# Where an attention pair's operand preparation stands in three instruction streams

## The chip, the cores and the metric

The kernel runs on one core of one Trainium2 chip. The metric is the device time of one execution in microseconds. Each core has a matmul engine (PE, with its weight loads PEld), VectorE (DVE), ScalarE (ACT), GpSimd (POOL) and a queue engine, SyncE (SP), which here only issues DMAs. Every engine works through its own instruction stream in order; semaphores join the streams.

## The reference

Causal attention with a decay, then a mixture of experts (one expert per token), then a two-layer network. Only the first part is touched by the change.

```python
B, H, S, D = q.shape                      # 4, 8, 576, 64
scores = scale * np.matmul(q, k.transpose(0, 1, 3, 2))
log_f = np.log(np.clip(f, 0.0001, 1.0))
cum = np.cumsum(log_f, axis=-1)
decay = cum[:, :, :, None] - cum[:, :, None, :]
causal = np.triu(np.ones((S, S), dtype=bool), k=1)
scores = np.where(causal, -1000000000.0, scores + decay)
scores = scores - np.max(scores, axis=-1, keepdims=True)
attn = np.exp(scores)
attn = attn / (np.sum(attn, axis=-1, keepdims=True) + 1e-09)
return np.matmul(attn, v).astype(np.float32)
# then: x = _moe_ref(x, ...); return _moe2_ref(x, w_in, w_out)
```

## The kernel before

The 32 heads are worked on in 16 **pairs** of heads, `g` = 0 to 15, in one loop of 17 turns. Turn `g` computes the scores of pair `g` and finishes pair `g-1`. Below, "pair 9" also means the turn that begins with pair 9's first scores.

**Operands.** The scores need about full single precision from a matmul that takes a rounded type, so each operand is split into a high part (rounded) and a low part (the rest). `raw` holds q in partitions 0 to 63 and k in 64 to 127. `prep_hi(g)` makes the high part on DVE (L299, `aq <- raw, qs`), issues two small loads of decay rows (L301, L302) and a copy of k's high part into `bk` (L303), all on SP, and two copies on POOL (L305). `prep_lo(g)` copies k's high part into the upper half of `ak` on ACT (L312, `ak <- aq`), makes the low part on DVE (L313, `raw <- raw, qs, aq`), issues three SBUF-to-SBUF DMAs of 288 KB on SP (L314 `bq <- raw`, L315 `ak <- raw`, L316 `aq <- aq`) and one copy on POOL (L317). L316 writes q's high part over the place where k's high part stood in `aq`, so it must come after L303, L312 and L313 have read it, and the first scores of that pair must wait until it has landed.

**One turn** is written as four stages, and with `ordered(tc, MS)` PE, ACT, DVE and SP keep the order in which they are written; POOL's order is set by a scheduler.

- `first(g)`: scores of query blocks 0 and 1 on PE and their maxima on DVE (L341, `nm`); transposes of pair g-1's block 3 on PE (L420, two PSUM tiles `pt`), their copies to SBUF on ACT (`cs`, L422); `prep_lo(g + 1)`; `store`, which issues finished rows of the attention output to DRAM on SP (L549, L551); the exponentials of blocks 0 and 1 on ACT (L346).
- `last(g)`: scores of the fifth, half block; the transposes of pair g-1's fifth block and their two copies on ACT (L412); pair g-1's first product with v (`pv`, L432) and its copy on DVE (L438); the fifth block's exponential on ACT (L393).
- `third(g)`: scores of block 2, the other `pv`, the exponentials of block 2, the transposes and copies of blocks 0 and 1.
- `fourth(g)`: scores of block 3; the loads of `raw` for pair g+3 (L202) and of `v` for pair g+1 (L193) on SP; `prep_hi(g + 2)`; transposes and copies of block 2; `xout(g - 1)`, the output stage; the exponentials of block 3.

`xout` scales pair g-1's output. It has two halves: matmuls into a PSUM tile `xo` (L455), then on DVE two products that read it (L459, into `x` and `lp`).

**PSUM.** The tiles `pt`, `xo` and `rk` share three buffers in turn, so each needs the third tile before it to have been read. The second `pt` tile of block 3 takes the buffer of the first `xo`, and the first `pt` tile of the fifth block that of the second `xo`. The scores have two buffers `sc` in turn: block 2's scores wait for the exponentials of blocks 0 and 1, block 3's for those of the fifth block.

**Side work.** After each four pairs the tokens of one batch are routed to experts in many small DVE instructions (`routed`, lines 473 to 536), whose first ones run in turns 5, 9 and 13, and after that the batch's rows are stored, one `store` a turn: 513 KB (L551) in turns 7, 8, 11 and 12, 128 KB (L549) in turns 9 and 13. In turn 2, `gload(1)` issues six small loads (L166, L170 four times, L171), written between `first` and `last`.

Of the kernel before, what the change touches and what calls it, by code (L numbers as in the profile page):

```python
# [9 lines left out]
F32 = mybir.dt.float32  # L10
# [9 lines left out]
P = 128  # L20
# [53 lines left out]
def fused(ctx: ExitStack, tc, qk0, qk2, vp, f, mid, wg, mb, w1, w2, w_in, w_out, out):  # L74
    nc = tc.nc
# [70 lines left out]
    with tc.tile_pool(name="pst", bufs=PST, space=PSUM) as pst:  # L146
# [40 lines left out]
        ops = {}  # L187
# [17 lines left out]
        NBUF = 2  # L205
        bqs = [pre.tile([68, 2, S], F32R, name=f"bq{i}") for i in range(NBUF)]
        bks = [pre.tile([68, 2, S], F32R, name=f"bk{i}") for i in range(NBUF)]
# [86 lines left out]
        def prep_hi(g):  # L294
            raw = ops[g]
            aq, ak = (aqk.tile([P, 2, S], F32R, tag=n, name=f"{n}{g}") for n in ("aq", "ak"))
            h = aq.bitcast(F32)
            bq, bk, a4, b4 = bqs[g % NBUF], bks[g % NBUF], aq4[g % NBUF], bq4[g % NBUF]
            nc.vector.tensor_scalar(aq, raw, qs, None, ALU.mult)  # L299
            for t, r0, c0 in ((bq, 64, 0), (bk, 66, 2)):  # L300
                nc.sync.dma_start(t[r0:r0 + 2].bitcast(F32), agd[c0:c0 + 2, 2 * g:2 * g + 2, :])  # L301
            nc.sync.dma_start(b4[64:66, :, :64].bitcast(F32), agd[0:2, 2 * g:2 * g + 2, 4 * P:])  # L302
            nc.sync.dma_start(bk[0:64].bitcast(F32), h[64:128])  # L303
            for r in (0, 64):
                nc.gpsimd.tensor_copy(a4[r:r + 64, :, :64], h[0:64, :, 4 * P:])  # L305
            ops[g] = (raw, aq, ak)

        def prep_lo(g):
            raw, aq, ak = ops[g]
            bq, bk, b4 = bqs[g % NBUF], bks[g % NBUF], bq4[g % NBUF]  # L310
            h = aq.bitcast(F32)
            nc.scalar.copy(ak[0:64], h[64:128])  # L312
            nc.vector.scalar_tensor_tensor(raw.bitcast(F32R), raw, qs, h, ALU.mult, ALU.subtract)  # L313
            nc.sync.dma_start(bq[0:64].bitcast(F32), raw[0:64])  # L314
            nc.sync.dma_start(ak[64:128].bitcast(F32), raw[64:128])  # L315
            preps.append(nc.sync.dma_start(h[64:128], h[0:64]))  # L316
            nc.gpsimd.tensor_copy(b4[0:64, :, :64], raw[0:64, :, 4 * P:])  # L317
            ops[g] = (aq, bq, ak, bk)

        st = {}  # L320
        XA, XB = 3 * P, P + 64
# [81 lines left out]
        def tr(g, c, js):  # L403
            sb = part_of(g, c // 3)
            if c == 4:
                pt = st.pop((g, c, "p"))
                for b0, b1 in ((0, 3), (3, 5)):
                    ps = pst.tile([P, 512], F32, tag="t", name=f"pt{g}_4_{b0}")
                    for b in range(b0, b1):
                        nc.tensor.transpose(ps[:, (b - b0) * P:(b - b0 + 1) * P], pt[:, b * P:(b + 1) * P], ident)  # L410
                    i = ps[:, :(b1 - b0) * P].rearrange("p (b j q) -> p j b q", j=2, q=64)
                    nc.scalar.copy(sb[:, :, b0:b1, P:], i)  # L412
                return
            pt = st[g, c, "p"]
            ps = pst.tile([P, 512], F32, tag="t", name=f"pt{g}_{c}_{js[0]}")
            nb = c + 1
            for i, j in enumerate(js):
                for b in range(nb):
                    k = i * nb + b
                    nc.tensor.transpose(ps[:, k * P:(k + 1) * P], pt[:, j, b * P:(b + 1) * P], ident)  # L420
            o = sb[:, js[0]:js[-1] + 1, 0:nb, c % 3 * P:(c % 3 + 1) * P]
            return lambda: nc.scalar.copy(o, ps[:, :len(js) * nb * P].rearrange("p (j b q) -> p j b q", b=nb, q=P))  # L422
# [14 lines left out]
            st[g, "x", part] = xu  # L437
            nc.vector.tensor_copy(xu[:, :w], pv_[:, :w])  # L438

        def xout(g):  # L440
            b, gg = divmod(g, H // 2)
            if gg == 0 and b:
                xt[b] = (pe, pre)[b % 2].tile([P, NC, XW], F32, tag="x", name=f"x{b}")
            x = xt[b]
            lp = lps[b % 2]
            rr = a3.tile([P, NC, 2], F32, tag="rr", name=f"rr{g}")

            nc.vector.tensor_copy(sms[g % 3][:64, 4, 1:2], sms[g % 3][64:, 4, 0:1])
            nc.vector.tensor_scalar(rr, sms[g % 3], 1e-9, None, ALU.add)
            nc.vector.reciprocal(rr, rr)  # L450
            for part, c0, n in ((0, 0, 3), (1, 3, 2)):
                xu = st.pop((g, "x", part))
                ps = pst.tile([P, 512], F32, tag="t", name=f"xo{g}_{part}")
                for i in range(n):
                    nc.tensor.matmul(ps[:, i * HW:(i + 1) * HW], lhsT=xu[:, i * P:(i + 1) * P], rhs=idw[:, gg, :], start=True, stop=True)  # L455
                i0 = ps[:, :n * HW].rearrange("p (c d) -> p c d", d=HW)
                sc = rr[:, c0:c0 + n, :].unsqueeze(3)
                for o, a, w in ((x[:, c0:c0 + n, gg * P:(gg + 1) * P], slice(0, P), D), (lp[:, c0:c0 + n, gg, :], slice(P, HW), E)):
                    nc.vector.tensor_tensor(o.rearrange("p c (j d) -> p c j d", j=2), i0[:, :, a].rearrange("p c (j d) -> p c j d", j=2), sc.to_broadcast([P, n, 2, w]), ALU.mult)  # L459
            if gg == H // 2 - 1:  # L460
                routing.append(route(b))
                if b == B - 2:
                    routing.append(route1(pre, (B - 1) * NC))
# [179 lines left out]
        NG = BH // 2  # L643
# [4 lines left out]
        def routed(n=1):  # L648
            for _ in range(n):
                if routing and next(routing[0], 1):  # L650
                    routing.pop(0)


        def first(g):
            then = qk01(g) if g < NG else None
            cs = [tr(g - 1, 3, (j, )) for j in range(2)] if g else ()
            if g + 1 < NG:
                prep_lo(g + 1)
            store(1 + (g > 12))
            for c in cs:  # L660
                c()
            for _ in then or ():
                pass

        def last(g):
            then = qk4(g) if g < NG else None
            if g:
                tr(g - 1, 4, (0, 1))
                routed()
                pv(g - 1, 0)  # L670
                routed(2 + (g > 12))
            if then:
                then()
# [12 lines left out]
        def fourth(g):  # L686
            then = qk(g, 3) if g < NG else None
            if g + 3 < NG:
                load(g + 3)
            if g + 1 < NG:  # L690
                vload(g + 1)
            if g + 2 < NG:
                prep_hi(g + 2)
            cs = [tr(g, 2, (j, )) for j in range(2)] if then else ()
            for c in cs:
                c()
            if g:
                xout(g - 1)
            if then:
                then()  # L700

# [530 lines left out]
```

## Time and profile before

| | us |
|---|---|
| median of 3 runs | 893.01 |
| lowest and highest | 888.86, 893.55 |
| the profiled execution, its own time | 889.86 |
| its span, first to last instruction | 888.2 |

The attention pairs lie in the first 205 us or so, the experts and the last network behind them. Times in the rows are microseconds from the first instruction of the span. A row of the time line has the start, the duration, the engine, the line, what is written and read with its size, and how many instructions are merged; in brackets stands the idle time of the engine before it and who ended it.

### The profile page before, as it was taken

Reading aid. Unit: us, or ns where it says so; the run is one execution under the profiler, and the core shown is the slowest. Engines: PE = TensorE matmul, PEld = TensorE weight load, DVE = VectorE, ACT = ScalarE, POOL = GpSimd, SP = SyncE. Lnnn points to the kernel's source line nnn. Section 1 sums busy time; section 2 is a strip of 40 time slices with the busy share of each in tenths; the row PEclk is TensorE's granted clock in tenths of the full one; section 3 lists DMA queues with packets and bytes.
Section 4 is the critical chain, followed back from the end, with each engine's and each line's share of the span. In section 5 each row is a group of like instructions: output and inputs, shape, how many; then the busy total and the mean of one; then the engine's idle time right before and its main releaser. Section 6 shows DMA issues by size and latency. Waiting matters only on the chain. (4 is left out here: it accounts for less than half of the span.)

```text
span 888.2 us, 14348 instructions
## 1 busy us (share of the span) xinstructions
PE 853.8 (96%) x4733; PEld 704.4 (79%) x4733; DVE 601.7 (68%) x1070; ACT 503.7 (57%) x969; POOL 124.9 (14%) x185
## 2 busy tenths in 40 slices
PE   5999999998999999999999999999999999999996
PEld 4788787886788788888787788888888888888885
DVE  6678777886748999999985373386337943473333
ACT  5787778776348899999975353453223422242221
POOL 5000000001112314532231000000000000001112
PEclk9999999999999999999999999999999999999998
DMA  5776786766278145121322240032001300011111
GB/s 153 222 175 183 204 201 180 203 174 221 74 229 285 53 155 166 55 71 51 107 96 64 59 143 13 1 106 84 1 1 48 119 24 0 1 48 48 48 47 72
DMA packets 32994, 92.91 MB, mean 105 GB/s; under 512 B 7349, under 2 KB 8021, under 8 KB 32914
## 3 DMA queue, kind: packets, MB, share of 16 engines
q1 hardware_dynamic: 28082, 76.70, 29.8%
q0 software_dynamic: 4800, 15.23, 5.4%
q8 instruction: 39, 0.64, 0.3%
q14 instruction: 41, 0.34, 0.1%
q10 hardware_dynamic: 32, 0.01, 0.0%
HBM read 132.09 MB, written 14.99 MB: 166 GB/s over the span
## 5 line engine op out<-in xcount | busy, mean ns | idle before, releaser
L1124 ACT COPY us<-u 128x512 f32<-128x512 f32 (+1 forms) x80 | 43.6, 544 | 162.6 <-PE u L1122 162.5
L1125 DVE SCALAR_TENSOR_TENSOR us<-u,us 128x512 f32<-128x512 f32 (+1 forms) x80 | 51.0, 638 | 124.7 <-ACT us L1124 123.1
L1122 PE MATMUL u<-fxl,whii 128*128 128x512 f32 (+1 forms) x320 | 118.0, 369 | 0.0
L1122 PE MATMUL u<-fxh,wloi 128*128 128x512 f32 (+1 forms) x320 | 117.9, 368 | 0.0
L1122 PE MATMUL u<-fxh,whii 128*128 128x512 f32 (+1 forms) x320 | 116.8, 369 | 0.7 <-ACT fxh L764 0.7
L1142 PE MATMUL a<-whio,gh 128*128 128x512 f32 x280 | 109.6, 392 | 0.0
L1142 PE MATMUL a<-wloo,gh 128*128 128x512 f32 x280 | 109.2, 390 | 0.0
L1142 PE MATMUL a<-whio,gl 128*128 128x512 f32 x280 | 103.2, 389 | 0.0
L876 DVE TENSOR_TENSOR w1l<-w1r,w1h 128x1024 fp32r<-128x1024 f32 x72 | 86.3, 1221 | 10.8 <-ACT w1h L875 8.3
L346 ACT ACTIVATE p<-sc,nm 128x128 f32<-128x128 f32 (+3 forms) x128 | 66.2, 527 | 28.9 <-DVE nm L341 27.2
L876 DVE TENSOR_TENSOR w2l<-w2r,w2h 128x1024 fp32r<-128x1024 f32 x68 | 80.2, 1218 | 0.8 <-ACT w2h L875 0.7
L1127 ACT CAST gh<-us 128x512 fp32r<-128x512 f32 (+1 forms) x76 | 44.6, 587 | 58.1 <-DVE us L1125 38.5
L875 ACT CAST w1h<-w1r 128x1024 fp32r<-128x1024 f32 x72 | 73.7, 1055 | 3.6 <-PE h L893 3.6
L1128 DVE TENSOR_TENSOR gl<-us,gh 128x512 fp32r<-128x512 f32 (+1 forms) x76 | 49.3, 648 | 38.5 <-ACT gh L1127 36.4
L875 ACT CAST w2h<-w2r 128x1024 fp32r<-128x1024 f32 x68 | 69.5, 1052 | 4.4 <-PE y L921 2.3
L1122 PEld LDWEIGHTS u<-fxh,whii 128*128 128x128 f32 x320 | 60.2, 188 | 11.0 <-ACT fxh L764 0.9
L1122 PEld LDWEIGHTS u<-fxh,wloi 128*128 128x128 f32 x320 | 60.3, 188 | 10.3
L1122 PEld LDWEIGHTS u<-fxl,whii 128*128 128x128 f32 x320 | 60.3, 188 | 10.3
L341 DVE TENSOR_REDUCE nm<-sc 128x2 f32<-128x256 f32 (+1 forms) x64 | 51.1, 820 | 23.4 <-PE sc L337 21.3
L921 PE MATMUL y<-w2h,hh 128*128 128x512 f32 x160 | 64.8, 405 | 0.0
L1152 POOL DMA_INDIRECT out<-acc,tid x18 | 18.0, 997 | 326.0 <-DVE acc L1149 287.5
L921 PE MATMUL y<-w2h,hl 128*128 128x512 f32 x160 | 63.1, 395 | 0.2 <-DVE hl L914 0.2
(275 smaller groups left out, 1807.6 us busy)
## 6 DMA issues: line engine op xcount, KB each, us to landing
w1r<-w SPq DMA_DIRECT2D x88, 512.0 KB
w2r<-w SPq DMA_DIRECT2D x82, 512.0 KB
rwi<-w_in SPq DMA_DIRECT2D x16, 512.0 KB
rwo<-w_out SPq DMA_DIRECT2D x16, 512.0 KB
raw<-qk SPq DMA_DIRECT2D x14, 576.0 KB
vt<-vp SPq DMA_DIRECT2D x16, 320.0 KB
xr<-yd SPq DMA_DIRECT2D x18, 256.5 KB
bk<-aq SPq DMA_DIRECT2D x15, 288.0 KB
```

Source lines behind the costliest of these rows:

```text
L341: nc.vector.tensor_reduce(nm, view, axis=AX.X, op=ALU.max, negate=True)
L346: st["exp"] = nc.scalar.activation(pt[:, j, :], view[:, j, :], AF.Exp, bias=nm[:, j:j + 1], scale=1.0, accum_out=sms[g % 3][:, c, j:j + 1])
L875: nc.scalar.copy(hi[k], raw[k])
L876: nc.vector.tensor_tensor(lo[k], raw[k], hi[k].bitcast(F32), ALU.subtract)
L921: nc.tensor.matmul(Yp[t], lhsT=ap[:, k * P:(k + 1) * P], rhs=wp[k // 2][:, k % 2, :], start=(k == 0 and i == 0), stop=(k == NFB - 1 and i ...
L1122: nc.tensor.matmul(ps, lhsT=w[:, c], rhs=x[:, k, :], start=(k == 0 and i == 0), stop=(k == NKB - 1 and i == 2))
L1124: nc.scalar.copy(us, ps)
L1125: nc.vector.scalar_tensor_tensor(us, ps, 0.01, us, ALU.mult, ALU.max)
L1127: nc.scalar.copy(gh, us)
L1128: nc.vector.tensor_sub(gl, us, gh.bitcast(F32))
L1142: nc.tensor.matmul(A[b][i], lhsT=x[:, c], rhs=w, start=(first and m == 0), stop=(last and m == 2))
L1152: d = nc.gpsimd.indirect_dma_start(out=out[:, :], out_offset=bass.IndirectOffsetOnAxis(ap=tid[:, c:c + 1], axis=0), in_=Y[b, i], in_offset ...
```

## The change

The diff changes no instruction, only where three pieces of `prep_hi` and `prep_lo` stand:

1. `prep_lo` is parted. A new `prep_k` holds the ACT copy of `ak` and the DMA `aq <- aq`. For pairs 1 and 2 it follows `prep_lo` directly; for pairs 3 to 15 it stands in `last`, behind the copies of the fifth block.
2. From turn 2 on, `prep_lo` stands behind the copies `cs` of block 3.
3. `prep_hi(g + 2)` stands between the two halves of `xout(g - 1)`, where it stood ahead of both.

```diff
@@ prep_lo @@
-            nc.scalar.copy(ak[0:64], h[64:128])
             nc.vector.scalar_tensor_tensor(raw.bitcast(F32R), raw, qs, h, ALU.mult, ALU.subtract)
             nc.sync.dma_start(bq[0:64].bitcast(F32), raw[0:64])
             nc.sync.dma_start(ak[64:128].bitcast(F32), raw[64:128])
+            nc.gpsimd.tensor_copy(b4[0:64, :, :64], raw[0:64, :, 4 * P:])
+
+        def prep_k(g):
+            raw, aq, ak = ops[g]
+            h = aq.bitcast(F32)
+            nc.scalar.copy(ak[0:64], h[64:128])
             preps.append(nc.sync.dma_start(h[64:128], h[0:64]))
-            nc.gpsimd.tensor_copy(b4[0:64, :, :64], raw[0:64, :, 4 * P:])
-            ops[g] = (aq, bq, ak, bk)
+            ops[g] = (aq, bqs[g % NBUF], ak, bks[g % NBUF])
...
-        def xout(g):
+        def xout(g, between=None):
...
+                if part == 0 and between:
+                    between()
@@ first @@
-            if g + 1 < NG:
+            if g < 2:
+                prep_lo(g + 1)
+                prep_k(g + 1)
+            for c in cs:
+                c()
+            if 2 <= g < NG - 1:
                 prep_lo(g + 1)
             store(1 + (g > 12))
-            for c in cs:
-                c()
@@ last @@
                 tr(g - 1, 4, (0, 1))
+                if 2 <= g < NG - 1:
+                    prep_k(g + 1)
                 routed()
                 pv(g - 1, 0)
@@ fourth @@
-            if g + 2 < NG:
-                prep_hi(g + 2)
             cs = [tr(g, 2, (j, )) for j in range(2)] if then else ()
             for c in cs:
                 c()
+            hi = (lambda: prep_hi(g + 2)) if g + 2 < NG else None
             if g:
-                xout(g - 1)
+                xout(g - 1, hi)
+            elif hi:
+                hi()
```

On ACT, turn 2 before (from the exponentials of block 3 of pair 1 on; numbers at the end of names are buffers):

```order
L346 ACTIVATE p_3_530,sm_185<-sc_3_483,nm_3_490 128x512 x2
L312 CAST ak_497<-aq_496 64x1152
L422 COPY tt_1_548<-pt_3_0_549 128x4x128
L422 COPY tt_1_548<-pt_3_1_554 128x4x128
L346 ACTIVATE p_01_567,sm_186<-sc_01_533,nm_0_544 128x128 x2
L346 ACTIVATE p_01_567,sm_186<-sc_01_533,nm_1_546 128x256 x2
L412 COPY tt_1_548<-pt_4_0_590 128x2x3x64
L412 COPY tt_1_548<-pt_4_3_595 128x2x2x64
L393 ACTIVATE p_177,sm_186<-sc_4_578,nm_4_579 128x576
```

and after (lines behind the edit count some lines further):

```order
L350 ACTIVATE p_3_530,sm_185<-sc_3_483,nm_3_490 128x512 x2
L426 COPY tt_1_548<-pt_3_0_549 128x4x128
L426 COPY tt_1_548<-pt_3_1_554 128x4x128
L350 ACTIVATE p_01_565,sm_186<-sc_01_533,nm_0_544 128x128 x2
L350 ACTIVATE p_01_565,sm_186<-sc_01_533,nm_1_546 128x256 x2
L416 COPY tt_1_548<-pt_4_0_588 128x2x3x64
L416 COPY tt_1_548<-pt_4_3_593 128x2x2x64
L320 CAST ak_517<-aq_516 64x1152
L397 ACTIVATE p_177,sm_186<-sc_4_576,nm_4_577 128x576
```

The copy of `ak` has moved past eight instructions, to just ahead of the fifth block's exponential.

On DVE, from the maxima of block 3 in turn 2 to the low part in turn 3, before:

```order
L341 TENSOR_REDUCE nm_3_651<-sc_3_644 128x2
L299 TENSOR_SCALAR aq_657<-raw_492,qs 128x1152
L448 COPY sm_185<-sm_185 64x1
L449 TENSOR_SCALAR rr_676<-sm_185 128x10
L450 RECIPROCAL rr_676<-rr_676 128x10
L459 TENSOR_TENSOR x_209<-xo_0_680,rr_676 128x3x128
L459 TENSOR_TENSOR lp_191<-xo_0_680,rr_676 128x3x16
L459 TENSOR_TENSOR x_209<-xo_1_686,rr_676 128x2x128
L459 TENSOR_TENSOR lp_191<-xo_1_686,rr_676 128x2x16
L341 TENSOR_REDUCE nm_0_705<-sc_01_694 128x2
```

and after:

```order
L345 TENSOR_REDUCE nm_3_651<-sc_3_644 128x2
L452 COPY sm_185<-sm_185 64x1
L453 TENSOR_SCALAR rr_667<-sm_185 128x10
L454 RECIPROCAL rr_667<-rr_667 128x10
L463 TENSOR_TENSOR x_209<-xo_0_671,rr_667 128x3x128
L463 TENSOR_TENSOR lp_191<-xo_0_671,rr_667 128x3x16
L299 TENSOR_SCALAR aq_677<-raw_492,qs 128x1152
L463 TENSOR_TENSOR x_209<-xo_1_686,rr_667 128x2x128
L463 TENSOR_TENSOR lp_191<-xo_1_686,rr_667 128x2x16
L345 TENSOR_REDUCE nm_0_705<-sc_01_694 128x2
```

The high part (`aq`) now stands between the products of the first and of the second `xo`; all else keeps its order.

On SP, the end of `prep_lo` in turn 2, before:

```order
L314 DMA bq_174<-raw_350 64x1152
L315 DMA ak_497<-raw_350 64x1152
L316 DMA aq_496<-aq_496 64x1152
L166 DMA mbs<-mb 128x16
L170 DMA midi<-mid 128x4x2 x4
L171 DMA midi<-mid 64x4x2
L202 DMA raw_653<-qk 128x1152
```

and after:

```order
L313 DMA bq_174<-raw_350 64x1152
L314 DMA ak_517<-raw_350 64x1152
L166 DMA mbs<-mb 128x16
L170 DMA midi<-mid 128x4x2 x4
L171 DMA midi<-mid 64x4x2
L321 DMA aq_516<-aq_516 64x1152
L202 DMA raw_653<-qk 128x1152
```

`aq <- aq` (L316 before, L321 after) now stands behind `gload`'s six loads. In the six turns that store, it likewise stands behind the store, as in turn 7 before:

```order
L315 DMA ak_1333<-raw_1153 64x1152
L316 DMA aq_1332<-aq_1332 64x1152
L551 DMA xs<-x_209 128x2x513
L202 DMA raw_1484<-qk 128x1152
L193 DMA vt_1486<-vp 128x640
```

and after:

```order
L314 DMA ak_1353<-raw_1153 64x1152
L557 DMA xs<-x_209 128x2x513
L321 DMA aq_1352<-aq_1352 64x1152
L202 DMA raw_1484<-qk 128x1152
L193 DMA vt_1486<-vp 128x640
```

The store and `aq <- aq` have changed places. On PE and, apart from the copy of `ak`, on ACT nothing else moves; the order of POOL's copies is as before.

## Rows read from the trace of the kernel before

**Rows 1.** The page, busy time, share and instructions of PE over the span.

```profile
PE 853.8 (96%) x4733; PEld 704.4 (79%) x4733; DVE 601.7 (68%) x1070; ACT 503.7 (57%) x969; POOL 124.9 (14%) x185
```

**Rows 2.** Time line of PE, starts of stages in pairs 7, 8 and 9.

```profile
97.16 0.32 PE L331 MATMUL sc<-ak,aq 128*128 128x128 f32 x1
...
98.39 1.04 PE L420 MATMUL pt<-ident,p 128*128 128x128 f32 x8
99.18 0.51 PE L383 MATMUL sc<-ak,aq 128*128 128x288 f32 x2
...
108.66 0.32 PE L331 MATMUL sc<-ak,aq 128*128 128x128 f32 x1
...
120.58 0.32 PE L331 MATMUL sc<-ak,aq 128*128 128x128 f32 x1
...
121.80 0.60 PE L420 MATMUL pt<-ident,p 128*128 128x128 f32 x4
122.62 0.63 PE L420 MATMUL pt<-ident,p 128*128 128x128 f32 x4 [0.22 <-DVE lp L459]
123.00 0.52 PE L383 MATMUL sc<-ak,aq 128*128 128x288 f32 x2
...
126.68 0.44 PE L331 MATMUL sc<-ak,aq 128*128 128x384 f32 x1 [0.30 <-ACT p L346]
```

**Rows 3.** Waits of PE from 20 to 195: total us, times, longest.

```profile
PE pt L420 <- DVE lp L459: 2.0, 8, 0.4
PE sc L331 <- DMA aq<-aq: 1.4, 2, 0.9
PE sc L331 <- ACT p L346: 1.2, 4, 0.3
```

**Rows 4.** Time line of DVE in pair 9.

```profile
120.18 0.81 DVE L299 TENSOR_SCALAR aq<-raw,qs 128x1152 fp32r<-128x1152 f32 x1
...
122.27 0.20 DVE L459 TENSOR_TENSOR lp<-xo,rr 128x48 f32<-128x48 f32 x1
...
123.86 1.01 DVE L341 TENSOR_REDUCE nm<-sc 128x2 f32<-128x256 f32 x2
```

**Rows 5.** Time line of ACT in pair 9.

```profile
121.77 1.15 ACT L312 CAST ak<-aq 64x1152 fp32r<-64x1152 f32 x1
...
124.90 0.37 ACT L346 ACTIVATE p<-sc,nm 128x128 f32<-128x128 f32 x1 [1.02 <-DVE nm L341]
...
129.14 0.58 ACT L346 ACTIVATE p<-sc,nm 128x384 f32<-128x384 f32 x1 [1.13 <-DVE nm L341]
```

**Rows 6.** Time line of SP in pair 2, issues of `prep_lo` and `gload`.

```profile
41.81 0.74 SPq L316 DMA_DIRECT2D aq<-aq  x1
...
43.90 3.57 SPq L170 DMA_DIRECT2D midi<-mid  x4
47.52 0.71 SPq L171 DMA_DIRECT2D midi<-mid  x1
```

**Rows 7.** Time line of PE, first scores of pair 3.

```profile
48.24 0.30 PE L331 MATMUL sc<-ak,aq 128*128 128x128 f32 x1
```

**Rows 8.** Time line of SP in pair 8.

```profile
114.48 0.73 SPq L316 DMA_DIRECT2D aq<-aq  x1
115.26 1.24 SPq L551 DMA_DIRECT2D xs<-x  x1
```

**Rows 9.** DMA traffic from 113 to 121, all queues.

```profile
DMA packets 560, 1.65 MB, mean 206 GB/s; under 512 B 65, under 2 KB 65, under 8 KB 559
```

**Rows 10.** Busy times from 195 to 212; the last figure is DMA's GB/s.

```profile
195.00:212.00 17.00, 13.92 (x119) 10.84 (x117) 13.41 (x45) 13.15 (x34) 2.24 (x2) 1.00 0.84 301
```

**Rows 11.** Time line of SP in pair 0, the issue for pair 1.

```profile
19.19 0.46 SPq L316 DMA_DIRECT2D aq<-aq  x1
```

**Rows 12.** Time line of PE, first scores of pairs 1 and 14.

```profile
23.35 0.30 PE L331 MATMUL sc<-ak,aq 128*128 128x128 f32 x1 [0.95 <-DMA aq<-aq]
...
182.58 0.30 PE L331 MATMUL sc<-ak,aq 128*128 128x128 f32 x1 [0.43 <-DMA aq<-aq]
```

## The prediction

> **What bounds the kernel now.** The page comes first: PE is busy 96% of the span [rows 1], so what shortens the time is a wait of PE, and the change touches the attention pairs alone. Next the time line of PE, read by the first scores of each pair. Pair 7 runs from 97.16 to 108.66, 11.50 us, with no wait marked at the places shown; I take that as what PE needs. Pair 8 runs to 120.58, 11.92 us, 0.42 more [rows 2]. Where the 0.42 lies is seen one pair later, in the same stage: the eight transposes of block 3 take 0.79 us in pair 7 (98.39 to 99.18) and 1.20 in pair 9 (121.80 to 123.00), since the second four wait for DVE's product `lp`, which frees their PSUM buffer. The row calls 0.22 of this idle; start to start it is 0.41, and that is the price I use [rows 2].
>
> Then PE's waits by cause [rows 3]. Three kinds bear on the change. The wait for `lp` comes 8 times (pairs 2, 5, 6, 8, 9, 10, 12, 13). The wait of block 2's scores for ACT's exponentials comes 4 times; pair 9 shows one of 0.30 [rows 2]. The wait for the DMA `aq <- aq` (L316) comes twice, at the first scores of pairs 1 and 14. The last says that this DMA lands close to when it is needed.
>
> **The high part between the output halves (DVE).** The high part takes 0.81 us and stands ahead of the products; the first `lp` ends at 122.47 [rows 4]. Behind it, `lp` ends near 121.66, and the second four transposes could start at 121.80 + 0.40 = 122.20. The wait is gone, 0.41 in each of 8 pairs, 3.3 us at most. The second half's `lp` ends when it did, since DVE does the same work up to there, and its taker stands behind the fifth block's scores, which begin at 122.59 at the soonest: no new wait. The high part itself ends about 1.4 us later, and with it L303 and POOL's two copies; they are needed one pair (11.5 us) later, and SP has nothing behind L303 until the low part is made: nothing.
>
> Not all of the 3.3 reaches the end. In pairs 5, 9 and 13 routing lengthens DVE's stretch: the maxima of blocks 0 and 1 end at 124.87 [rows 4], the exponentials start at 124.90 after an idle 1.02 [rows 5], and block 2's scores wait for them until 126.68 [rows 2]. DVE's sum up to the maxima is unchanged, so PE would wait 0.71 there instead of 0.41 + 0.30: nothing gained. In pairs 6 and 10, which still do routing, I keep half, 0.2 each (an estimate). Pair 2 ends in another wait (below): nothing. Pairs 8 and 12 keep 0.41 each, if nothing else holds the next pair.
>
> **The copy of `ak` (ACT).** It takes 1.15 us. In pair 9 it stood where ACT then idled 1.02 anyway; now it stands where ACT idled 1.13 ahead of block 2's exponentials [rows 5]. The cover is 0.02 short; what those exponentials release (transposes) comes two PE stages later, so I cost it at nothing; without cover it would be 0.1 a pair over 13 pairs, 1.3 us. The copies of block 3 come about 1 us sooner, but the exponentials behind them wait for DVE: nothing, and below nothing only where DVE is early.
>
> **The DMA `aq <- aq` (SP).** This is where I expect the loss. It is now issued when the copy of `ak` has ended, about 1.1 us later than before in a plain pair (the copy's own 1.15), and behind whatever is written between. How near is it to its need? The only issue with little else queued ahead is pair 0's: issued at 19.19 [rows 11], released PE at 23.35 [rows 12], 4.16 us. In pair 8 it was issued at 114.48 [rows 8]; 4.16 us later is 118.64, and PE needed it at 120.58, so there the slack is at most 1.94 and, as no wait shows, at least 0. In the plain pairs (3 to 6, 10, 14) a delay of 1.1 fits into the upper end, and the two DMAs queued ahead of it delay its landing anyway: I take nothing, at most 0.4 in each of six pairs.
>
> *Pair 2.* SP issues `gload`'s six loads from the end of L316 to 48.23, about 5.6 us [rows 6]. L316, at 41.81 before, comes near 47.4; plus 4.16 is 51.6, and pair 3 began at 48.24 [rows 7]: 3.3 us lost. At the other end the four `midi` issues (3.57 us) go 1 us faster without L316's bytes ahead, and the landing takes 3 us on an empty queue (both estimates): 1.2 us. I take 2.0, nearer the lower end, since six loads of a few KB leave the queue empty. Pair 2's own 0.41 is swallowed by this wait.
>
> *Pairs 7, 8, 11, 12.* A store of 513 KB (0.525 MB) now goes ahead of L316. At the 301 GB/s of a dense stretch [rows 10] that moves L316 by 1.75 us, at the 206 GB/s of pair 8 [rows 9] by 2.55. In pair 8 the landing is then between 118.64 + 1.75 = 120.39 and 120.58 + 2.55 = 123.13, and without the `lp` wait it is needed at 120.17: PE waits 0.2 to 3.0, less the 0.41 gained, so -0.2 to +2.5; I take 1.1. In pairs 7 and 11 there is no 0.41 to gain and the low part is made earlier in the pair; I take half, 0.6. A late start gives DVE and ACT time that the next pair uses, 0.3 for each two. So 1.4 for pairs 7 and 8 and 1.4 for 11 and 12, together 2.8.
>
> *Pairs 9 and 13.* Started late, they find DVE ahead, and their 0.71 of waits shrinks; I take 0.6 off, and 0.1 back for the 128 KB stores (0.44 us at 301 GB/s) that now go ahead of L316: -0.5 each, -1.0. Pair 13 bounds this: its landing held pair 14 by 0.43 before [rows 12], and stays as near.
>
> **The sum.** +2.0 (pair 2) + 2.8 (large stores) - 1.0 (pairs 9, 13) - 0.4 (pairs 6, 10) = +3.4 us; the gain of pairs 8 and 12 is inside the 2.8. From about 212 on PE is the busy engine to the end, so I pass the sum on unchanged. On the profiled execution, 889.86, this gives 893.3. That run lies low among the runs shown (888.86 to 893.55, mean 891.8); on the mean it gives **895.2 us**.
>
> [...]
>
> **The rivals.**
>
> *Nothing lands late.* The slack before L316 is near its upper end, 1.94 in pair 8, and the small loads hold SP less long than they did. Then the gains stand alone: 0.41 in pairs 8 and 12, 0.2 in 6 and 10, and perhaps 0.41 in pair 2, -1.6 us, 890.2. For it: only two waits on this DMA in 14 pairs [rows 3]. Against it: 0.95 and 0.43 where they stand, and 5.6 us of issue in pair 2. Chance 0.20.
>
> [...] Chance 0.20.
>
> *The change doesn't do what it says.* The wait for the first `lp` turns into one for the second, which now has the high part ahead of it. Then the gains (0.4, and 0.8 inside the 2.8) go: +4.6, 896.4. Against it: DVE's sum up to the second `lp` is unchanged. Chance 0.06.
>
> **How the numbers follow.** The forecast has 0.54. Its terms at their lower ends (1.2 in pair 2, 0 for the stores, -1.0, -0.4) give about 0, at middling upper ends (3.3, 5.0, -1.0, -0.4) +6.9: 891.8 to 898.7. The range for 8 in 10 takes in part of both rivals and the runs' own scatter of 2 us either way: 889.5 to 901.0. 0.5%, about what a measurement of this kernel can tell from no change, is 4.5 us, so slower means over 896.3: nearly all of the second rival and a fifth of the rest, 0.30. Faster needs -4.5 us, more than all 3.3 of the `lp` waits together: 0.04. The same: 0.66.
>
> **What would show it.** In the profile of the changed kernel the wait for `lp` should be gone from PE's waits, and the one for `aq <- aq` grow from 2 times to 5 or more, at the first scores of pairs 3, 8, 9, 12 and 13, the largest at pair 3 with about 2 us. SP should issue this DMA near 47 in pair 2, and right behind the store in pair 8. Block 2's exponentials should start no more than 0.1 us after their maxima. Pairs without store or `gload` should take 11.5 us, pairs 9 and 13 near 12. I am wrong if PE shows no wait for the DMA (first rival), if pairs 7, 8, 11 and 12 are each over 2 us longer (second), or if the transposes of the fifth block wait for DVE (third).

## The result

The changed kernel takes 899.41 us in the median of 6 runs (898.59 to 901.63); the kernel before, in runs beside it, 892.85 (888.86 to 893.55). The ratio is 1.0087 with a 95% interval of 1.0063 to 1.0111: slower by 0.9%, some 7.8 us (the ratio is one of means; the medians lie 6.6 us apart). Forecast were 895.2 us and a range of 889.5 to 901.0; the time lies in the range, on the side that had a chance of 0.30.

The profiled run of the changed kernel took 898.59 us with a span of 896.3, against 889.86 and 888.2 before. So 8.1 of 8.7 us lie in the span. PE is as busy as in [rows 1], 96%:

```profile
PE 856.8 (96%) x4733; PEld 709.0 (79%) x4733; DVE 601.2 (67%) x1070; ACT 505.2 (56%) x969; POOL 117.6 (13%) x185
```

Where the 8.1 us are is read from the first scores of each pair, in the time line of PE of the changed kernel (start, duration, then what PE did; in brackets the idle time ahead and what ended it). A pair's length is the distance to the next row.

```profile
23.43 0.45 PE L335 MATMUL sc<-ak,aq 128*128 128x128 f32 x1 [2.00 <-DMA aq<-aq]
37.98 0.32 PE L335 MATMUL sc<-ak,aq 128*128 128x128 f32 x1
53.09 0.33 PE L335 MATMUL sc<-ak,aq 128*128 128x128 f32 x1 [3.25 <-DMA aq<-aq]
66.33 0.32 PE L335 MATMUL sc<-ak,aq 128*128 128x128 f32 x1
...
102.96 0.32 PE L335 MATMUL sc<-ak,aq 128*128 128x128 f32 x1
116.40 0.30 PE L335 MATMUL sc<-ak,aq 128*128 128x128 f32 x1 [1.67 <-DMA aq<-aq]
129.20 0.30 PE L335 MATMUL sc<-ak,aq 128*128 128x128 f32 x1 [0.94 <-DMA aq<-aq]
141.15 0.32 PE L335 MATMUL sc<-ak,aq 128*128 128x128 f32 x1
...
165.98 0.33 PE L335 MATMUL sc<-ak,aq 128*128 128x128 f32 x1 [0.54 <-DMA aq<-aq]
178.34 0.30 PE L335 MATMUL sc<-ak,aq 128*128 128x128 f32 x1 [0.52 <-DMA aq<-aq]
...
202.28 0.32 PE L335 MATMUL sc<-ak,aq 128*128 128x128 f32 x1
```

The last row is pair 15. Before, that pair began at 194.16; from there to the end of PE's last matmul both kernels take the same (685.72 before, 685.75 after). All but 0.08 us of the loss is in pairs 1 to 14, which is where PE's waits from 20 to 203 changed. They answer to [rows 3]:

```profile
PE sc L335 <- DMA aq<-aq: 9.1, 7, 3.2
PE sc L335 <- ACT p L350: 1.0, 3, 0.7
```

The wait for `lp` (2.0 us in eight) is gone. The wait for `aq <- aq` has grown from 1.4 us in 2 to 9.1 in 7. The waits alone don't give the pair lengths, though: pair 1 (23.43 to 37.98, 14.54 us against 12.44) and pair 3 (53.09 to 66.33, 13.24 against 11.82) are longer *behind* their wait, not ahead of it. The busy times of two stretches show why. The columns are the stretch, its length, busy time of PE, PEld, DVE, ACT and POOL with instructions, PE's granted clock, the share and GB/s of the DMA engines. Before:

```profile
23.00:30.00 7.00, 6.08 (x46) 4.81 (x47) 4.39 (x7) 5.58 (x17) 0.87 (x3) 1.00 0.96 307
53.00:60.00 7.00, 7.00 (x63) 5.72 (x60) 4.75 (x12) 4.61 (x15) 0.00 (x0) 1.00 0.94 250
```

After:

```profile
23.00:30.00 7.00, 6.57 (x30) 6.36 (x31) 3.47 (x5) 4.54 (x13) 0.86 (x3) 0.51 0.92 302
53.00:60.00 7.00, 6.91 (x44) 5.93 (x44) 3.11 (x4) 3.94 (x13) 0.29 (x1) 0.76 0.66 192
```

From 23 to 30 the granted clock is 0.51, from 53 to 60 it is 0.76. Read by single microseconds it is 0.50 from 24 to 29 and 1.00 from 30 on, and again 0.50 from 54 to 57 and 1.00 from 58 on. From 23 to 30, in the same part of pair 1, PE was busy longer and got 30 matmuls done where it did 46. (From 53 to 60 the two kernels are in different parts of pair 3, so there only the clock compares; over the whole of pair 3 it is 0.87, and 1.00 before.) The idle time ahead of the two falls was 2.00 and 3.25 us.

Last, SyncE's queue. In pair 2 (answers to [rows 6]), pair 7 and pair 8 (to [rows 8]), by the issues of DMAs:

```profile
44.95 4.00 SPq L170 DMA_DIRECT2D midi<-mid  x4
...
49.82 0.55 SPq L321 DMA_DIRECT2D aq<-aq  x1
...
108.03 0.82 SPq L557 DMA_DIRECT2D xs<-x  x1
109.42 1.29 SPq L321 DMA_DIRECT2D aq<-aq  x1
...
122.95 1.28 SPq L321 DMA_DIRECT2D aq<-aq  x1
```

The lengths of the pairs, from the time lines of PE (us; the columns on the right are experiments told below, under the names "all DMAs", "`gload` alone", "stores alone" and "best"):

| pair | before | after | all DMAs | `gload` alone | stores alone | best |
|---|---|---|---|---|---|---|
| 1 | 12.44 | 14.54 | 12.32 | 13.21 | 13.14 | 12.32 |
| 2 | 12.45 | 15.12 | 11.95 | 11.90 | 15.04 | 11.90 |
| 3 | 11.82 | 13.24 | 11.73 | 11.74 | 14.43 | 11.82 |
| 4 | 11.78 | 11.50 | 11.50 | 11.53 | 11.49 | 11.50 |
| 6 | 12.68 | 12.55 | 12.55 | 12.56 | 12.55 | 12.55 |
| 7 | 11.50 | 13.44 | 11.50 | 13.36 | 11.50 | 11.50 |
| 8 | 11.91 | 12.80 | 11.52 | 13.14 | 11.50 | 11.66 |
| 9 | 12.61 | 11.95 | 12.58 | 12.04 | 12.58 | 12.39 |
| 10 | 12.66 | 12.54 | 14.20 | 12.53 | 14.04 | 12.53 |
| 11 | 11.51 | 12.30 | 11.51 | 12.05 | 11.51 | 11.50 |
| 12 | 11.91 | 12.36 | 12.61 | 12.84 | 12.11 | 11.89 |
| 13 | 13.30 | 12.36 | 11.95 | 11.94 | 12.38 | 12.92 |
| 1 to 14 together | 170.81 | 178.85 | 170.20 | 173.14 | 176.46 | 168.69 |

The last line is the measure I trust most within one profile: the rest of the kernel, from pair 15 on, is the same code everywhere and still took 684.1 to 689 us up to PE's last matmul in the profiled runs.

### The profile page after: what moved, and what is told of

It is laid out like the page before. It is cut to its first block, busy times and chain, and to the rows that moved or that the text cites. A ratio compares the mean times of both kernels' runs of the same rounds, so it can differ in the third digit from the quotient of the medians.

```text
span 896.3 us, 14336 instructions
## 1 busy us (share of the span) xinstructions
PE 856.8 (96%) x4733; PEld 709.0 (79%) x4733; DVE 601.2 (67%) x1070; ACT 505.2 (56%) x969; POOL 117.6 (13%) x185
## 5 line engine op out<-in xcount | busy, mean ns | idle before, releaser
L933 PE MATMUL y<-w2l,hh 128*128 128x512 f32 x160 | 62.5, 391 | 0.0
```

The costliest lines, as they stand in the source:

```text
L933: nc.tensor.matmul(Yp[t], lhsT=ap[:, k * P:(k + 1) * P], rhs=wp[k // 2][:, k % 2, :], start=(k == 0 and i == 0), stop=(k == NFB - 1 and i ...
```

## The experiments

Theory A: the loss is `aq <- aq` standing behind `gload` and the stores in SyncE's queue. Rival B: it is ScalarE's late copy of `ak`, whatever the queue does. Rival C: it is the high part between the halves. Later, theory E: a part of it is PE's clock. Each ratio is to runs of the kernel before on the same chip, with its 95% interval.

### The high part between the halves, alone

The kernel before with only this part of the diff:

```
-            if g + 2 < NG:
-                prep_hi(g + 2)
...
+            hi = (lambda: prep_hi(g + 2)) if g + 2 < NG else None
...
+                xout(g - 1, hi)
```

> The kernel before with the high part between the output halves, and nothing else: ak's copy, its DMA and the stores stand in first(g) as before. Theory A (the loss is the order of SyncE's queue: aq <- aq behind gload(1) and behind the stores): no wait for aq <- aq beyond the two of before (1.4 us in sum), the waits of the transposes for VectorE's lp (2.0 us in eight) gone or halved, time 0 to 2 us below the kernel before, pair 2 (from its first scores to those of pair 3) 12.4 us, pair 7 11.5. Rival C (the high part between the halves is what costs): 3 to 8 us above the kernel before, with pairs 2 and 7 longer than in before. Clock: no drop at pairs 1 and 3 by A, or at pair 1 alone if that one belongs to the run.

Measured: 891.12 us against 891.49, ratio 1.0002 (0.9987 to 1.0018). PE's waits from 20 to 203:

```profile
PE sc L331 <- ACT p L346: 4.4, 11, 0.6
PE sc L331 <- DMA aq<-aq: 2.4, 2, 1.7
```

Rival C falls: alone, the part costs nothing that the ratio shows. It brings nothing either. The wait for `lp` is gone, but the one for ScalarE's exponentials has grown from 1.7 us in 5 (the same stretch before) to 4.4 in 11, and pairs 8 and 9 take 11.94 and 12.58 us, as before. Pairs 2 and 7 came out as expected (12.32 and 11.50). Beside pair 1, of which more below, two pairs are longer: pair 12 (12.91 against 11.91), with a wait of 0.71 us for `aq <- aq` behind it, and pair 10 (13.33 against 12.66), where VectorE's product, which now comes sooner, has to wait for a store:

```profile
134.75 0.56 DVE L459 TENSOR_TENSOR x<-xo,rr 128x384 f32<-128x384 f32 x1 [0.73 <-DMA xs<-x]
```

PE now reaches block 2's scores sooner and waits there for the exponentials, which in this kernel still stand behind the copy of `ak`; the next experiment has them ahead of it.

### All DMAs in their old order, the copy late

The changed kernel with `gload(1)` and the stores moved behind `prep_k`:

```
             if 2 <= g < NG - 1:
                 prep_lo(g + 1)
-            store(1 + (g > 12))
...
                     prep_k(g + 1)
+                store(1 + (g > 12))
...
-                if g in (0, 2):
-                    gload(g // 2)
+                if g == 0:
+                    gload(0)
...
                     last(g)
+                    if g == 2:
+                        gload(1)
```

> The changed kernel with gload(1) and the stores issued behind prep_k, so that SyncE's queue has its old order, while ScalarE's copy of ak stays behind the exponentials. Theory A (order of the queue): the waits of the first scores of pairs 3, 8, 9, 12 and 13 for aq <- aq (9.1 us in seven in the changed kernel) gone but for pair 1's; pair 2 back from 15.12 to about 12.4, pairs 7, 8, 11, 12 back to 11.5, 11.9, 11.5, 11.9; time within 2 us of the kernel before or up to 2 below. Rival B (the late copy on ScalarE makes the release of the DMA late whatever stands in the queue): at least three of these waits stay, 4 to 8 us above the kernel before.

Measured: 890.95 us, ratio 1.0002 (0.9987 to 1.0018). The waits at pairs 3, 8, 9 and 12 are gone; one of 0.85 stays at pair 13, which I had not expected, and pair 12 stays at 12.60. Pairs 2, 7, 8 and 11 are back. So rival B falls: with the queue in its old order the late copy costs nothing, and with it the high part between the halves brings what it didn't bring alone (pairs 2 and 8 at 11.95 and 11.52, 0.50 and 0.39 less than before). The late copy alone, without that part and with the old order, was not run.

One thing was not expected: pair 10 takes 14.20. In its time lines VectorE's first product waits for a store, and PE then waits for VectorE:

```profile
133.47 0.56 DVE L463 TENSOR_TENSOR x<-xo,rr 128x384 f32<-128x384 f32 x1 [1.75 <-DMA xs<-x]
...
134.28 0.63 PE L424 MATMUL pt<-ident,p 128*128 128x128 f32 x4 [1.09 <-DVE lp L463]
```

This product, of pair 8, is the first of batch 2 and writes into the `x` buffer of batch 0, which the small store of turn 9 still reads. That store now goes out later, and the product comes sooner in the pair: it was ready at 131.72, 12.93 us into pair 9, and before it started 13.84 into it. It is the wait of 0.73 of the last experiment, made longer by the later store. The early place of the stores has a use, which I had not seen.

### `gload` alone, and the stores alone

The same edit in two halves; the first moves `gload(1)` behind `prep_k`, the second the stores.

> The changed kernel with gload(1) alone moved behind pair 2's aq <- aq on SyncE; the stores still stand ahead of theirs. Theory A: pair 2 back from 15.12 to about 12.4 us and pair 3 from 13.24 to 11.8 (its stretch at the half clock goes with the wait ahead of it), pairs 7, 8, 11, 12 as in the changed kernel (13.44, 12.80, 12.30, 12.36): 4 us below the changed kernel, 3 to 5 above the kernel before. Rival B (late copy): pair 2 stays near 15.1 and the time is that of the changed kernel within 1 us.

Measured: 896.19 us, ratio 1.0054 (1.0036 to 1.0073). First scores of pairs 3 and 4, then of 8 and 9:

```profile
48.66 0.30 PE L335 MATMUL sc<-ak,aq 128*128 128x128 f32 x1
60.41 0.32 PE L335 MATMUL sc<-ak,aq 128*128 128x128 f32 x1
...
110.44 0.30 PE L335 MATMUL sc<-ak,aq 128*128 128x128 f32 x1 [1.60 <-DMA aq<-aq]
123.58 0.30 PE L335 MATMUL sc<-ak,aq 128*128 128x128 f32 x1 [1.30 <-DMA aq<-aq]
```

> The changed kernel with the stores alone moved behind aq <- aq of their turn on SyncE; gload(1) still stands ahead of pair 2's. Theory A: pairs 7, 8, 11, 12 back to 11.5, 11.9, 11.5, 11.9 (4.1 us in sum), pairs 9 and 13 back to 12.6 and 13.3 at most (1.6 us given back), pair 2 still 15.1 with the half clock in pair 3: 2.5 to 4 us below the changed kernel. Rival B (late copy): the waits at the first scores of pairs 8, 9, 12 and 13 stay (3.7 us), the time is that of the changed kernel within 1 us.

Measured: 895.41 us, ratio 1.0058 (1.0037 to 1.0080). The same places, with SyncE's issue in pair 7 in the middle:

```profile
51.52 0.47 PE L335 MATMUL sc<-ak,aq 128*128 128x128 f32 x1 [3.17 <-DMA aq<-aq]
65.95 0.32 PE L335 MATMUL sc<-ak,aq 128*128 128x128 f32 x1
...
109.03 0.46 SPq L321 DMA_DIRECT2D aq<-aq  x1
...
114.07 0.32 PE L335 MATMUL sc<-ak,aq 128*128 128x128 f32 x1
125.57 0.32 PE L335 MATMUL sc<-ak,aq 128*128 128x128 f32 x1
```

Each half takes away its own waits and leaves the other's. Without `gload` ahead, pair 2 is back at 11.90 and pair 3 at 11.74; without the stores ahead, pairs 7 and 8 are back at 11.50. By the ratios the halves are worth 0.0033 and 0.0029, 2.9 and 2.6 us, each with about 2.7 us of uncertainty; the first was expected at 4, and its median doesn't show that much. The second loses some of its gain in pair 10 (14.04), by the wait just shown.

The issue in pair 7 says more. Here `aq <- aq` is issued 6.46 us after the pair's first scores (109.03 - 102.57), in the changed kernel too (109.42 - 102.96). The place behind the store did not delay the start of the issue: in the changed kernel SyncE was done with the store at 108.85 and began when ScalarE's copy of `ak` ended, at 109.39. Here PE began pair 8 without a wait, 5.04 us after the issue began; there it was released 6.98 after it, 1.94 us or more later. A part of this is in the issue itself, which took 1.29 us there and 0.46 here; the other 1.11 us lie between its end and the release.

### The changed kernel without the part between the halves

```
+            if g + 2 < NG:
+                prep_hi(g + 2)
...
-                xout(g - 1, hi)
+                xout(g - 1)
```

> The changed kernel without its third part: the high part stands again ahead of the output stage, ak's copy and its DMA stay late. Theory A (the loss is the queue of SyncE): the waits for aq <- aq at pairs 3, 8, 9, 12 and 13 stay within 0.5 us of the changed kernel's, the transposes' waits for lp come back (8 of 0.2 to 0.4 us) but mostly within waits that are there anyway, time 0 to 2 us above the changed kernel. Rival C (the part between the halves costs): 2 us or more below the changed kernel.

Measured: 900.16 us, ratio 1.0115 (1.0093 to 1.0137), by the ratios 2.5 us above the changed kernel, where 0 to 2 were expected. PE's waits:

```profile
PE sc L335 <- DMA aq<-aq: 6.0, 4, 2.2
PE pt L424 <- DVE lp L463: 1.1, 5, 0.2
```

The waits for the DMA stay at pairs 3, 8 and 13 (2.20, 1.67, 1.08); those at pairs 9 and 12 are gone, and only the one at pair 8 is within the expected 0.5 us of the changed kernel's. Pair 8 took 13.33 us in this run, with PE busy throughout and the granted clock at 0.87:

```profile
113.31:126.64 13.33, 13.33 (x98) 11.40 (x99) 7.06 (x11) 8.71 (x24) 0.29 (x1) 0.87 0.72 190
```

I take it that the slower pair gave pair 9's DMA its time, but nothing was run to show it. Rival C falls a second time: without the part the kernel is not faster.

### Small stores kept ahead: a version that beats both

As the second experiment, but only the large stores go behind:

```
+            if g in (9, 13):
+                store(1 + (g > 12))
...
                     prep_k(g + 1)
+                if g not in (9, 13):
+                    store(1 + (g > 12))
```

> The changed kernel with gload(1) and the large stores (turns 7, 8, 11, 12) behind aq <- aq, and the small stores of turns 9 and 13 ahead of it. Theory A with its second part (pair 10 was long, 14.20 and 14.04 us where both kinds stood behind, since VectorE's first write of a new x buffer waited 1.75 us for the last small store that reads it): pair 10 back from 14.2 to 12.6, VectorE's wait for xs <- x gone, no other wait back, 1.6 us below the run with all DMAs in their old order and 2 to 4 us below the kernel before (median 887.5 to 889.5 against 891.5). Rival D (the 1.75 us go elsewhere: the small store ahead delays aq <- aq of turns 9 and 13 by as much): pairs 9 or 13 grow by 0.5 us or more, time that of the run with all DMAs in their old order within 0.7 us.

Measured: 888.39 us against 890.59, ratio 0.9975 (0.9960 to 0.9991), 2.2 us faster than the kernel before and about 2.4 less (by the ratios, with some 2 us of uncertainty) than with all DMAs in their old order. Pair 10 is back at 12.53, and the same product of VectorE waits for nothing, so the wait for the `x` buffer was what pair 10 had lost:

```profile
132.07 0.56 DVE L463 TENSOR_TENSOR x<-xo,rr 128x384 f32<-128x384 f32 x1
```

Pairs 1 to 14 take 168.69 us, 2.1 less than before. Rival D named the price of the small stores: pair 9 did not grow, pair 13 did (12.92 against 11.95 where the small store stands behind), while pair 12 shrank by 0.72, so the two together moved by 0.25.

### Matmuls in the waits

The changed kernel, with work for PE while it waits for `aq <- aq` ahead of pairs 1 and 3:

```
+            for _ in range({1: 12, 3: 25}.get(g, 0) if c == 0 else 0):
+                nc.tensor.matmul(view, lhsT=identb, rhs=trimask..., start=True, stop=True)
             one = c < 2
```

> The changed kernel with extra matmuls ahead of the first scores of pairs 1 and 3 (12 and 25 of 256 columns, into the scores' own PSUM tile, which the scores then start anew), so that PE works while it waits for aq <- aq; nothing else is moved. Theory E (1.4 to 2.6 us of pair 3 and 0.9 to 2.1 of pair 1 are the granted clock at its lower level behind the wait, not more waiting): granted clock 1.00 from 23 to 60 us, pair 1 12.4 and pair 3 11.8 us, pair 2 still 15.1, time 2 to 4 us below the changed kernel. Rival F (the stretch at the lower clock is not tied to the idle time ahead of it): pairs 1 and 3 stay at 13.2 to 14.5 with the clock at 0.5 for some microseconds, time as the changed kernel or up to 0.5 above.

Measured: 894.17 us, ratio 1.0039 (1.0021 to 1.0056). PE between pairs 2 and 4, then the two stretches:

```profile
48.00 2.89 PE L334 MATMUL sc<-trimask,identb 128*128 128x256 bf16 x25
51.48 0.33 PE L337 MATMUL sc<-ak,aq 128*128 128x128 f32 x1 [0.59 <-DMA aq<-aq]
63.12 0.32 PE L337 MATMUL sc<-ak,aq 128*128 128x128 f32 x1
...
23.00:30.00 7.00, 5.88 (x46) 4.44 (x44) 3.86 (x6) 4.69 (x16) 0.86 (x3) 1.00 0.96 316
53.00:60.00 7.00, 7.00 (x64) 5.61 (x63) 5.94 (x13) 5.47 (x16) 0.29 (x1) 1.00 0.70 178
```

The granted clock is 1.00 in both, pair 1 takes 12.34 and pair 3 11.64 us, and pair 2 still takes 15.16: the release has not moved, only what came behind it. By the ratios that is 0.0048 less than the changed kernel, 4.3 us, with about 2.7 us of uncertainty. So theory E holds, and rival F falls: of the changed kernel's 7.8 us a part, about half by this figure, was the clock that fell behind these two waits. The clock of whole runs points the same way: 0.985 to 0.991 in the changed kernel's six, 0.992 to 0.998 in these eleven. But the kernel before has runs at 0.987 too (0.987 to 0.998 in 28 beside these eleven), and what the same matmuls would give it was not run. In the profiled run it fell at another place (0.97 from 105 to 155), behind the wait of 1.47 us at pair 9, which made that pair 13.63.

### The best version with matmuls in pair 1's wait

The sixth experiment's kernel (the "run before last" of the text) with 12 such matmuls ahead of pair 1's first scores.

> The kernel of the run before last (gload(1) and the large stores behind aq <- aq, the small stores ahead) with 12 extra matmuls of 256 columns ahead of pair 1's first scores. Theory E: granted clock 1.00 throughout pair 1 in every run, so the runs lose their upper group; 0.5 to 2 us below the same kernel without the extra matmuls in the median, 3 to 5 below the kernel before. Rival F: the median of the kernel without them within 0.5 us.

Measured: 889.75 us, ratio 0.9987 (0.9974 to 1.0001), above the 888.39 without them; the two intervals overlap. From 23 to 30 the clock is 1.00 here, but it was 1.00 without the extra matmuls too, and the runs still spread over 4 us. So this gains nothing that shows, and pair 1's clock is hardly what spreads the best version's runs; it was read in one profiled run of each kernel only.

### The store cut in halves, and the store on another queue

Two tests of why the stores delay the DMA, both on the changed kernel. The first cuts each large store in two and issues the second half behind `prep_k`; in the second GpSimd issues the stores.

```
+                    nc.sync.dma_start(xs[t0:t0 + P, :], x[:, c0, :])
+                    rest.append((t0 + P, x, c0 + 1, c1))
...
                     prep_k(g + 1)
+                store_rest()
```

> The changed kernel with the large stores cut in two DMAs: the first half (256 KB) ahead of aq <- aq, the second behind it; gload(1) stays ahead. Theory G (what delays aq <- aq is the data of the store that moves ahead of it on the same queue): half the data, half the delay: pair 7 from 13.44 to 12.4, pair 8 from 12.80 to 12.2, pairs 11 and 12 (12.30, 12.36) to 11.9 and 12.1; 1.5 to 2.5 us below the changed kernel. Rival H (what delays it is the place behind one more DMA on SyncE, its issue of 0.8 us): the waits stay within 0.3 us of the changed kernel's, the time too within 0.7 us.

Measured: 895.33 us, ratio 1.0053 (1.0026 to 1.0079). First scores of pairs 7 to 9:

```profile
102.90 0.32 PE L335 MATMUL sc<-ak,aq 128*128 128x128 f32 x1
115.58 0.30 PE L335 MATMUL sc<-ak,aq 128*128 128x128 f32 x1 [0.92 <-DMA aq<-aq]
127.18 0.32 PE L335 MATMUL sc<-ak,aq 128*128 128x128 f32 x1
```

SyncE's issue in pair 7:

```profile
109.36 1.07 SPq L321 DMA_DIRECT2D aq<-aq  x1
```

Pairs 7, 8, 11 and 12 take 12.68, 11.59, 11.78 and 12.06, together 48.11, against 50.90 in the changed kernel and 46.83 before: with half the data ahead, a third of the loss is left there. Pairs 9 and 13 (12.58 and 12.78) take back 1.05 us of the gain, since they start on time. By the ratios the kernel is 3.0 us below the changed one (1.5 to 2.5 expected). The number of DMAs ahead is the same, so less data means less delay, and rival H falls as it was put. In pair 7 the issue begins 6.46 us into the pair once more, and the release is late by 1.18 us, not 1.94: 0.61 of it is in the longer issue (1.07 against 0.46), where it was 0.83, and 0.57 behind it, where it was 1.11. The part behind the issue halves with the data (theory G); the longer issue shrinks by a quarter only, and what makes it longer no run separates.

```
-                    nc.sync.dma_start(xs[t0:...
+                    nc.gpsimd.dma_start(xs[t0:...
```

> The changed kernel with all stores issued by GpSimd in place of SyncE, at the same place in the program: the same data at about the same time, but on another queue. Theory G1 (the order within the one queue: aq <- aq moves when the store ahead of it has): pairs 7, 8, 11, 12 back to 11.5 to 11.9 us each, 3 to 4 us below the changed kernel. Rival G2 (the DMA engines are shared, whatever the queue): these pairs stay at 12.2 or more, the time within 1.5 us of the changed kernel.

Measured: 895.63 us, ratio 1.0048 (1.0025 to 1.0072). GpSimd's issue, and the first scores of pairs 7 and 8:

```profile
101.01 1.70 POOL L557 DMA_DIRECT2D xs<-x  x2 [4.81 <-DVE x L542]
...
103.20 0.32 PE L335 MATMUL sc<-ak,aq 128*128 128x128 f32 x1
114.70 0.32 PE L335 MATMUL sc<-ak,aq 128*128 128x128 f32 x1
```

The pairs are back (11.50, 11.50, 11.98, 11.60), near enough to what theory G1 expected, but the test doesn't tell G1 from G2: GpSimd issued both large stores as soon as `x` was ready, ahead of pair 7 and 9 us ahead of the issue of `aq <- aq` (110.14), so the stores no longer stood close ahead of it. Whether another queue at the same moment would have helped stays open.

## Why the prediction was right or wrong

**Right: where and why.** The wait for `lp` gone; waits for `aq <- aq` at the first scores of pairs 3, 8, 9, 12 and 13, the largest at pair 3; the DMA issued in pair 2 as late as forecast (11.84 us into the pair, which is 47.6 on the clock of the kernel before); the loss from the order of SyncE's queue, shown by the second to fourth experiments. The copy of `ak` at nothing holds as well: block 2's exponentials in pair 7 start behind VectorE, not behind the copy, and the second experiment shows no cost of the late copy. One sign did not come: pairs 5, 6 and 10, without store or `gload`, took 12.5 to 12.6 us and not 11.5.

```profile
108.24 1.15 ACT L320 CAST ak<-aq 64x1152 fp32r<-64x1152 f32 x1
...
110.49 0.58 ACT L350 ACTIVATE p<-sc,nm 128x384 f32<-128x384 f32 x1 [0.24 <-DVE nm L345]
```

**Pair 2: 2.0 forecast, 2.67 measured** (15.12 - 12.45), within its bounds of 1.2 to 3.3. The step that was off in its lower bound is that the four `midi` issues would go 1 us faster without `aq <- aq` ahead: they took 4.00 us, 0.43 *more* than the 3.57 of [rows 6]. From the issue at 49.82 to PE's start at 53.09 it was 3.27 us, near the 3 that I had estimated and under the 4.16 of pair 0.

**Pairs 7, 8, 11 and 12: 2.8 forecast, 4.07 measured** (1.94, 0.89, 0.79, 0.45). Here the step "in pairs 7 and 11 I take half" failed. I had thought that a pair without a wait for `lp`, whose low part is made earlier, has more room ahead of the landing. Pairs 7 and 11 lost 2.73 together, pairs 8 and 12 1.34: nearly the reverse of my 1.2 and 2.2 (before the 0.3 for each two). The earlier low part was so before, when the DMA was issued 5.01 us into pair 7 (the row below) and 5.82 into pair 8 [rows 8]. In the changed kernel it is issued behind the copy of `ak`, 6.46 and 6.55 us into these pairs, so pair 7 lost its lead.

```profile
102.17 0.73 SPq L316 DMA_DIRECT2D aq<-aq  x1
```

The room behind the issue was about the 5.04 us that the fourth experiment shows, and the release came 6.98 us after the issue in pair 7 (109.42 to 116.40) and 6.25 in pair 8 (122.95 to 129.20); why pair 8's was quicker no run tells. No run shows the term behind the second rival, on which most of the 0.30 for slower rests. In its place the runs showed a release that is later the more data is ahead (in pair 7 by 1.18 us or more for half the store and by 1.94 or more for all of it, the longer issues included), and none of the four pairs was over 2 us longer, which was that rival's mark.

**Pairs 9 and 13: -1.0 forecast, -1.60 measured** (-0.66 and -0.94). **Pairs 6 and 10: -0.4 forecast, -0.25 measured.** Pair 4 gave 0.28 that I had not counted. Together with the two terms above this makes +4.6 against a sum of +3.4; the signs are all as forecast.

**Wrong by omission: the clock.** Pair 1 (+2.10) and pair 3 (+1.42) are 3.5 us for which the forecast has no term. I read every wait as its own length and left PE's clock at 1.00, since [rows 7] and the pairs of [rows 2] gave no cause to look; that the change would put new idle time ahead of PE's work was cause enough. The granted clock was 0.77 over pair 1 and 0.87 over pair 3, and the experiment with matmuls in the waits, with 1.00 in both stretches and pairs of 12.34 and 11.64 us, shows that the 3.5 us in the profile are the clock's.

Pair 3's share stands behind a wait that the change made. Pair 1's share is not shown to be the change's. No order of work ahead of its first scores is edited, and they start at nearly the same time (23.35 before, 23.43 after). The wait was 0.95 before and is 2.00 now because PE had finished pair 0 sooner: its last six transposes began at 20.61 and took 0.83 us, against 21.23 and 1.17.

```profile
21.23 1.17 PE L420 MATMUL pt<-ident,p 128*128 128x128 f32 x6
...
20.61 0.83 PE L424 MATMUL pt<-ident,p 128*128 128x128 f32 x6
```

Of the ten profiled kernels without extra matmuls there, the clock fell in pair 1 of six (0.51 to 0.76 from 23 to 30; the pair took 13.1 to 14.6 us) and stayed at 1.00 in four (12.3 to 12.6), the kernel before among them. So the +2.10 may be the luck of this one run; the kernel before has whole runs at a clock of 0.987 as well, over 5 us above its fastest. It was luck, too, that the time fell into the range: 899.41 is above the 898.7 of the forecast's own upper ends, and the room above that was made for the second rival and the runs' scatter; the clock used it.

**Also missed:** that the stores' early place frees the `x` buffer. I had costed the small stores at 0.1 us for standing ahead; standing behind they cost 1.5 in pair 10.

The forecast's terms as measured, +4.6, and the clock's +3.5 make +8.1, which is the span's +8.1. Without the clock the forecast's terms do better: the changed kernel with matmuls in both waits stands 3.5 us above the kernel before (1.9 to 5.0). The chance of 0.30 for slower is a little under what its own words make it, about 0.34.

## What to carry to other kernels

A DMA that is moved behind a compute step is moved past everything that is issued in between; count the data ahead of it in its queue, not only the issues (in pair 7 513 KB ahead made the release 1.94 us later or more, half of it 1.18 or more), and look first at the pair whose lead the move takes away (here pair 7, issued 6.46 us into it and not 5.01). When a forecast adds a wait to TensorE, add a term for the clock that may fall behind it (here to 0.51 and 0.76 over 7 us, behind 2.00 and 3.25 us of idle time), and read the granted clock by stretch, not only over the span. Before a store is moved later, look for who writes next into the buffer that it reads (here that write waited 1.75 us).

## What the runs showed of the hardware

In pair 1, from 23 to 30, the granted clock was 0.51 behind an idle time of 2.00 us (changed kernel) and 0.76 behind 1.74 (high part alone), but 1.00 behind the 2.23 of the kernel with all DMAs in their old order, at the same place in the program. Ahead of pair 8 the same idle time of 1.67 us left it at 1.00 in the changed kernel and was followed by 0.87 over the pair in the kernel without the part between the halves. So the length of the one wait does not settle it, and what does stays open. With matmuls in the wait, which then was 0.83 us, it stayed at 1.00. The row of the kernel with all DMAs in their old order, and that of the kernel with the high part alone:

```profile
23.12 0.30 PE L335 MATMUL sc<-ak,aq 128*128 128x128 f32 x1 [2.23 <-ACT p L350]
...
22.91 0.30 PE L331 MATMUL sc<-ak,aq 128*128 128x128 f32 x1 [1.74 <-DMA aq<-aq]
```

A store of 513 KB ahead of `aq <- aq` made its release in pair 7 1.94 us later or more, and half of it 1.18 or more, though SyncE began that issue no later: 6.46 us into the pair in all three kernels. The issue itself took 1.29 us behind the whole store, 1.07 behind half of it, and 0.46 with the store behind.
